# A new order of the opening work list: output-weight quarters in order of use, then the next group's keys and queries, then the values

## The chip, the cores and the metric

The kernel runs on one core of one Trainium2 chip. Its time is the device time of one execution in microseconds (us), given as the median over several executions. Five engines take part, each with its own instruction stream that runs in order: TensorE (PE, matrix products), VectorE (DVE), ScalarE (ACT, exponentials and GELU), GpSimd (POOL, masks and a part of the loads) and SyncE (SP, loads of values and stores of results). They meet only in semaphores.

## The reference

Attention with a forget gate, then a two-layer MLP. There are 8 batches, 8 heads, 576 positions, head size 64; the MLP goes from 512 to 2048 to 512 on all 4608 tokens. All inputs and the output are float32.

```
scores = scale * q @ k^T                      # per batch and head
cum    = cumsum(log(clip(f, 1e-4, 1)))
scores = where(causal, scores + cum[:, None] - cum[None, :], -1e9)
attn   = softmax(scores) @ v
x      = attn, heads side by side             # 4608 x 512
out    = gelu_tanh(x @ w_in) @ w_out
```

## The kernel before

**Attention.** Four heads form a quad; there are 16, two for each batch. The decay depends on query and key only through a factor of the key that can be pulled into the values: `make_vw` (L231) multiplies the values of a quad by exp(-cum) and writes the tile `vw`, in bfloat16. For a quad, `load_one` (L208, words LK and LQ of the lists) loads k and q with a cast to bfloat16 on POOL's DMA queue, `transpose_words` (L214, TK and TQ) transposes them on DVE, `scores` (L277, word S) multiplies them on PE in three rounds and lets ACT take the exponential into the tile `pt` (L285). Then the part of `pt` above the diagonal is set to zero, either on POOL by an affine select (L291, word M) or on DVE by a product with a 0/1 tile (L321, word m). `denominators` (word D) forms the row sums on PE (L347) and their reciprocals on DVE (L366 to L370), and `attn_out` (word V, two products for each quad) multiplies `pt` by `vw` on PE and by the reciprocals on DVE into `xT` (L379). A quad's products also need a copy of the first 64 key rows of `vw` in its last slot, at partitions 64 to 127; `copy_low` (L236, word CL) makes this edge-row copy on DVE. Tiles of k, q, `pt` and `vw` are held in two copies, for even and for odd quads.

**MLP.** Tokens go in nine chunks of 512. Words J, I, E and Q form x @ w_in and the GELU. The first chunk's second product is plain (`mlp_out`, L667, words F.0.n and f.0.n): for each of four groups of 128 tokens it adds 16 products over the rows of `w_out_sb` into a bank of PSUM (the tile `pso`), copies the bank to SBUF on DVE (L672) and stores it from SP. One word F.0.n is n of these 64 products; F uses the whole array at a time, f the same work in four strips of 32 columns. Later chunks use a scheme with seven products in place of eight on sums of blocks (L600, words F.1.n and on), for which DVE forms sums of `w_out_sb` (L567, word U), of the activations (L578 to L584, word G) and of `w_in_sb` (L450 and L452, word UW).

**Order.** There is no automatic order: `run` walks through a written list of words (`FRONT` for the first two chunks, then other lists), and each word emits its instructions, which keep that order on each engine. `@` behind a word adds a wait: the word's first load starts only when the named word's instruction is done. `load_w_out` (L201, words WO.0 to WO.3) loads a quarter of `w_out_sb`, four of the sixteen row blocks in the order in which `mlp_out` uses them, with a cast, on POOL's queue. The values of batch 1 come in five pieces of 128 positions (words LC.1.0 to LC.1.4, L185) on the same queue; those of batch 2 (words LV.2.0, LV.2.1) come on SP's queue. The words vw and VW are `make_vw` on DVE and on POOL; a second figure names a part. X loads the exponential's table on ACT.

The pools that bear on the order: `pso` lies in a pool of two banks, so the third group of 128 tokens needs the first one's copy done; the row sums and the two products of a quad share one PSUM tile (`psO`, one copy), so each needs the reader of the one before to be done.

```
psO = ctx.enter_context(tc.tile_pool(name="psO", bufs=1, space=bass.MemoryType.PSUM))
psM = ctx.enter_context(tc.tile_pool(name="psM", bufs=2, space=bass.MemoryType.PSUM))
...
def copy_low(i):
    return nc.vector.tensor_copy(vw[i % 2][64:128, LOW], vw[i % 2][0:64, 0])
...
for (key, col, q0, nq) in sorted(pieces, key=lambda x: {0: 0, "low": 1}.get(x[0], 2)):
```

The last line sets the order of the key blocks in D and V: block 0, then the edge rows, then the rest.

Of the kernel before, what the change touches and what calls it, by code (L numbers as in the profile page):

```python
# [16 lines left out]
def kernel(  # L17
# [841 lines left out]
```

## Time and profile before

| what | value |
|---|---|
| median of 3 executions | 325.47 us (323.58 to 325.6) |
| the profiled execution | 326.56 us, of which the span from first to last instruction is 324.3 us |
| PE busy | 310.0 us, 96% of the span |
| DVE, ACT, POOL busy | 241.7, 212.6, 107.0 us |
| granted TensorE clock | 1.000 of full speed |
| PE waiting for `w_out_sb` | 1.3 us in two waits |
| TK, TQ transpose on DVE | 1.25 us each |
| edge-row copy on DVE | 0.22 us each |

Times in the profile are counted from the start of the span. In a row of the timeline stand its start, its length, the engine, the line of the kernel, the operation, output<-inputs with shapes, and how many instructions are merged; in brackets the idle time of the engine before it and what ended that idle time. Matmuls are pipelined, so the length shown for a group on PE overlaps the next group by some 0.1 us.

### The profile page before, as it was taken

The numbers are of one execution on the slowest core, as the hardware profiler recorded it, in microseconds if no ns is written. First come the engines' busy times: TensorE is split into PE (matmuls) and PEld (weight loads), VectorE is DVE, ScalarE is ACT, GpSimd is POOL, SyncE is SP. The second block draws the span as 40 slices with busy tenths as digits, with TensorE's granted clock in tenths as the row PEclk, the third lists the DMA queues.
The fourth block names the chain that finished last, engine by engine and source line by source line (L and its number), as shares of the span: only waits on it lengthen the run. The fifth ranks groups of instructions, "written<-read, shape, count | busy, mean of one in ns | idle before, by whom it ended". The sixth has DMA issues, their size and how long they took to land.

```text
span 324.3 us, 11816 instructions
## 1 busy us (share of the span) xinstructions
PE 310.0 (96%) x5337; PEld 221.2 (68%) x5337; DVE 241.7 (75%) x374; ACT 212.6 (66%) x242; POOL 107.0 (33%) x145
## 2 busy tenths in 40 slices
PE   0799989999999999999999999999999999999996
PEld 0557844454677667776788877767776786788785
DVE  3664307998989978779876998599885866597574
ACT  4495667686766786678667876877587743846610
POOL 8868507253111405510752056305610150000000
PEclk9999999999999999999999999999999999999999
DMA  6999999577034951395119610981001011010202
GB/s 117 232 155 165 196 250 217 139 160 143 8 67 88 227 116 36 76 213 107 36 40 211 143 40 6 206 183 35 7 32 67 17 35 53 16 50 2 99 33 98
DMA packets 47490, 33.41 MB, mean 103 GB/s; under 512 B 29776, under 2 KB 42192, under 8 KB 47440
## 3 DMA queue, kind: packets, MB, share of 16 engines
q0 software_dynamic: 9632, 15.99, 28.4%
q1 hardware_dynamic: 37664, 16.60, 18.9%
q8 instruction: 41, 0.67, 0.8%
q14 instruction: 9, 0.07, 0.1%
q10 hardware_dynamic: 144, 0.07, 0.1%
HBM read 36.85 MB, written 9.44 MB: 143 GB/s over the span
## 4 chain that ended last, share of the span: by engine, by line
PE 82%; DMA 6%; POOL 4%; ACT 4%; DVE 2%; issue 1%; POOLq 0%; DVEq 0%
PE ps_w L600 30%; PE ps_h L395 19%; PE po L347 9%; PE ps_q L520 8%; PE ps_s L277 8%; DMA w_out_sb<-in_moe_w_out_dram 4%; PE ps_u L468 4%; PE pso L667 4%; DMA q_c<-in_q_dram 2%; ACT pt L285 2%; POOL pt L291 1%; POOL w_out_sb L201 1%; POOL v_nat L185 1%; POOL w_in_sb L197 1%; PE cum_ps L721 1%
## 5 line engine op out<-in xcount | busy, mean ns | idle before, releaser
L285 ACT ACTIVATE pt<-ps_s 128x1024 bf16<-128x1024 f32 (+2 forms) x100 | 93.9, 990 | 41.3 <-PE ps_s L277 37.1
L291 POOL TENSOR_SCALAR_AFFINE_SELECT pt<-pt 128x512 bf16<-128x512 bf16 (+3 forms) x65 | 40.8, 639 | 98.0 <-ACT pt L285 75.2
L395 PE MATMUL ps_h<-xT,w_in_sb 128*128 128x512 bf16 (+1 forms) x320 | 66.8, 358 | 0.3 <-ACT gT L403 0.2
L395 PEld LDWEIGHTS <-w_in_sb 128*128 128x128 bf16 x320 | 31.2, 98 | 26.7 <-issue 0.6
L600 PEld LDWEIGHTS <-gT 128*32 128x32 bf16 (+1 forms) x1216 | 44.2, 97 | 5.5 <-issue 2.2
L403 ACT ACTIVATE gT<-ps_h 128x1024 bf16<-128x1024 f32 x34 | 34.6, 1017 | 18.7 <-PE ps_h L395 18.4
L600 PE MATMUL ps_w<-w_out_sb,gT 128*32 128x256 bf16 (+1 forms) x1008 | 42.6, 273 | 0.0
L277 PE MATMUL ps_s<-qT,kT 32*128 32x64 bf16 (+5 forms) x896 | 36.3, 263 | 4.6 <-DVE qT L214 4.3
L600 PEld LDWEIGHTS <-gsum 128*32 128x32 bf16 (+1 forms) x948 | 35.5, 97 | 3.6 <-issue 1.3
L231 POOL TENSOR_TENSOR vw<-v_nat,wT 128x1280 bf16<-128x1280 f32 (+1 forms) x13 | 29.6, 2278 | 11.8 <-DMA v_nat<-in_v_dram 11.5
L536 DVE TENSOR_TENSOR usnap<-ps_q,usnap 128x1024 f32<-128x1024 f32 x15 | 17.9, 1222 | 18.6 <-PE ps_q L520 13.2
L277 PEld LDWEIGHTS <-kT 32*128 32x128 bf16 x896 | 16.5, 93 | 20.9 <-issue 11.5
L600 PE MATMUL ps_w<-usum,gsum 128*32 128x256 bf16 (+1 forms) x791 | 29.9, 273 | 0.0
L617 DVE COPY snap<-ps_w 128x512 f32<-128x512 f32 x32 | 21.8, 681 | 6.1 <-PE ps_w L600 6.0
L531 ACT ACTIVATE gT<-usnap 128x1024 bf16<-128x1024 f32 x15 | 15.8, 1054 | 12.1 <-DVE usnap L536 11.8
L379 DVE TENSOR_TENSOR xT<-po,rb 128x576 bf16<-128x576 f32 x26 | 19.5, 752 | 5.6 <-PE po L347 5.3
L347 PE MATMUL po<-pt,vw 128*32 128x64 bf16 (+4 forms) x624 | 22.4, 278 | 0.0
L214 DVE STREAM_TRANSPOSE qT<-q_c 128x576 f32<-128x576 f32 x16 | 19.8, 1247 | 2.7 <-DMA q_c<-in_q_dram 2.5
L214 DVE STREAM_TRANSPOSE kT<-k_c 128x576 f32<-128x576 f32 x16 | 19.5, 1248 | 3.1 <-DMA k_c<-in_k_dram 3.1
L347 PEld LDWEIGHTS <-vw 128*32 128x32 bf16 x672 | 14.8, 97 | 9.3 <-issue 2.8
L208 POOL DMA_DIRECT2D k_c<-in_k_dram x16 | 9.1, 569 | 33.7 <-DVE kT L214 17.4
L520 PEld LDWEIGHTS <-w_in_sb 128*128 128x128 bf16 x160 | 15.6, 98 | 2.5 <-issue 0.4
(134 smaller groups left out, 478.4 us busy)
## 6 DMA issues: line engine op xcount, KB each, us to landing
out_dram<-o_st SPq DMA_DIRECT2D x35, 256.0 KB, 2.3
k_c<-in_k_dram POOLq DMA_DIRECT2D x16, 288.0 KB, 5.2
q_c<-in_q_dram POOLq DMA_DIRECT2D x16, 288.0 KB, 6.2
v_nat<-in_v_dram SPq DMA_DIRECT2D x16, 256.0 KB, 5.3
v_nat<-in_v_dram SPq DMA_DIRECT2D x20, 128.0 KB, 4.9
v_nat<-in_v_dram POOLq DMA_DIRECT2D x8, 256.0 KB, 8.2
w_in_sb<-in_moe_w_in_dram POOLq DMA_DIRECT2D x8, 256.0 KB, 7.6
w_out_sb<-in_moe_w_out_dram POOLq DMA_DIRECT2D x4, 512.0 KB, 11.1
```

What stands on the lines that cost most here:

```text
L214: return nc.vector.transpose(out=dst.rearrange("p s c -> p (s c)").bitcast(FP32) .rearrange("p (t a) -> p a t", a=S // 32), in_=src.rearra ...
L231: return eng.tensor_mul(vw[i % 2][:, t0:t1], vb[:, t0:t1, h0:h0 + 4, :], wT[:, i, t0:t1, :].unsqueeze(3).to_broadcast([128, t1 - t0, 4, D]))
L277: nc.tensor.matmul(tiles[h // 2][:, h % 2, c0:c0 + nq], key_columns(i, key, h, c), qq[32 * h:32 * h + 32, q0:q0 + nq, c], start=(c == 0 an ...
L285: nc.scalar.activation(p[:, 2 * g:2 * g + 2, off:off + n], t[:, :, 0:n], AF.Exp, scale=scale)
L291: nc.gpsimd.affine_select(out=x, in_=x, compare_op=ALU.is_ge, fill=0.0, base=0, pattern=pattern, channel_multiplier=-1)
L347: nc.tensor.matmul(po[r0:r0 + w.shape[-1], 448 + q0:448 + q0 + nq], w, p[:, h, col:col + nq], start=(key in (0, "low")), stop=(key in ("lo ...
L379: nc.vector.tensor_mul(xT[:, 2 * u + x, r0 + s0:r0 + s1], po, rbs[i, part])
L395: nc.tensor.matmul(ph[:, j, n * cols:(n + 1) * cols], w_in_sb[:, dt, 128 * ft:128 * ft + 128], xT[:, dt, h0:h0 + cols], start=(dt == 0 and ...
L403: nc.scalar.activation(gelus(c, 2 * pr, 2), ph, AF.Gelu_apprx_tanh)
L520: nc.tensor.matmul(ps[:, k, HC * n:HC * n + HC], w[:, d, 128 * n:128 * n + 128], x[:, d, :], start=(first and n == 0 and d == 0), stop=(d ...
L600: nc.tensor.matmul(ps[c0:c0 + width, n, cols[0]:cols[1]], x[:, j, 128 * n + c0:128 * n + c0 + width], w[:, j, cols[0]:cols[1]], start=(fir ...
L617: copy(kept[name], ps)
```

## The change

Only the list `FRONT` changes. The four quarters of `w_out` are issued on POOL's queue in the order 0, 1, 2, 3 with no values between them; behind them come k and q of quad 3, and behind these the remaining four pieces of the values of batch 1 (before: quarter 0, values 2, quarters 2 and 1, values 0, quarter 3, values 1 and 3, then k and q of quad 3). TQ.3 moves ahead of the first group's copy on DVE, beside TK.3. The mask of quad 2's second round moves from DVE (m.2.1) to POOL (M.2.1) and stands, with the other masks of that quad, ahead of VW.3, which was ahead of them. CL.2 and CL.3 now follow D.2 together; before, CL.2 stood ahead of D.2 and CL.3 after V.2.1. The products of the first chunk (F.0.n, f.0.n) are cut in other portions between the attention's words. UW.2.1, UW.2.2, m.4.1, VW.4 and some words of the I group change place by a few words, and LV.3.1 waits for LQ.7 in place of LK.6.

```diff
         WI.7 LK.2 V.1.1.0 m.0.3.2 H.1.3.0 j.0.0 vw.0.1 H.1.3.1 LC.1.4 m.0.3.4 D.0.1 M.1.3 S.1.2 M.1.1 VW.1.1 V.0.0.1 WO.0 V.0.1.1 LC.1.2 D.1.1
-        WO.2@m.0.3.4 J.0.1 J.0.2 WO.1 LC.1.0@VW.1.1 WO.3@m.0.3.2 V.1.0.1 V.1.1.1 LC.1.1 GJ.0.0 LC.1.3 TK.2 J.1.1 LK.3 J.0.3 J.1.0 LQ.3 TQ.2 LQ.4 VW.3
-        J.1.3 LK.4 J.1.2 F.0.4 X F.0.4 S.2.0 F.0.11 TK.3 S.2.2 F.0.6 LV.2.0 TQ.3 F.0.4 LK.5 S.2.1 F.0.2 F.0.7 TQ.4 m.2.1 S.3.0 vw.2 CL.2 M.2.2 f.0.7
-        M.2.0 D.2 S.3.1 f.0.7 LQ.5 V.2.0 m.3.0 S.3.2 TK.4 LK.6@LQ.4 f.0.1 f.0.3 V.2.1 M.3.2 f.0.2 S.4.1 CL.3 m.3.1 LQ.6 f.0.5 TQ.5 H.4.2.1 D.3 H.4.0.1
-        H.4.0.0 VW.4 V.3.1 v.3.0 f.0.1 H.4.2.0 U.0 m.4.1 LV.2.1@m.3.1 I.1.1 LQ.7@CL.3 I.1.4 TQ.6 I.1.6 m.4.2.3 I.1.0 m.4.2.2 I.1.5 CL.4 U.3 LV.3.0@LQ.7
-        U.1 TK.6 I.1.2 M.4.0 U.2 G.0 TK.5 UW.2.1 I.1.3 I.1.7 G.1.1.2 F.1.16 X UW.2.2 S.5.0 UW.2.3 LQ.8 F.1.19 S.5.1 D.4 VW.5 M.5.0 f.1.13 S.5.2 V.4.0
+        ... V.0.0.1 WO.0 V.0.1.1 D.1.1 WO.1@m.0.3.4
+        J.0.1 J.0.2 WO.2 WO.3 LK.3 LQ.3 V.1.0.1 V.1.1.1 LC.1.2 LC.1.0@m.0.3.4 LC.1.3 GJ.0.0 LC.1.1 TK.2 J.1.1 J.0.3 TQ.2 J.1.0 J.1.3 LQ.4 LK.4 J.1.2
+        F.0.4 F.0.5 X TK.3 TQ.3 S.2.0 F.0.11 S.2.2 F.0.10 LV.2.0 LK.5 S.2.1 F.0.9 vw.2 S.3.0 TQ.4 F.0.8 M.2.2 M.2.0 M.2.1 D.2 VW.3 S.3.1 CL.2 CL.3 F.0.6
+        LQ.5 V.2.0 m.3.0 TK.4 S.3.2 LK.6@LQ.4 f.0.2 M.3.2 V.2.1 F.0.1 f.0.2 S.4.1 m.3.1 LQ.6 F.0.5 TQ.5 H.4.2.1 D.3 H.4.0.1 H.4.0.0 V.3.1 v.3.0
+        f.0.1 H.4.2.0 VW.4 m.4.1 U.0 LV.2.1@m.3.1 I.1.1 I.1.4 LQ.7@CL.3 UW.2.1 TQ.6 I.1.6 I.1.0 m.4.2.3 m.4.2.2 I.1.5 CL.4 U.3 LV.3.0@LQ.7 U.1 I.1.2
+        TK.6 M.4.0 U.2 I.1.3 I.1.7 G.0 TK.5 G.1.1.2 X UW.2.2 F.1.16 S.5.0 UW.2.3 LQ.8 F.1.19 S.5.1 D.4 VW.5 M.5.0 f.1.13 S.5.2 V.4.0 f.1.14 V.4.1
...
-        LV.3.1@LK.6 f.1.5 CL.6 LK.8 m.6.2.3
+        ... V.5.0 LV.3.1@LQ.7 f.1.5 CL.6 LK.8 m.6.2.3
```

More of the change, by code (lines that the diff above doesn't have):

```diff
@@ L77 @@
         WI.5 H.1.0.0 D.0.0 M.1.0.1 M.1.0.0 H.0.1.1 V.0.0.0 H.0.1.0 M.0.1 LQ.2 V.0.1.0 B.1.256 H.1.1.0 D.1.0 WI.4 H.0.3.0 WI.6 B.1.256 V.1.0.0 H.0.3.1
-        WI.7 LK.2 V.1.1.0 m.0.3.2 H.1.3.0 j.0.0 vw.0.1 H.1.3.1 LC.1.4 m.0.3.4 D.0.1 M.1.3 S.1.2 M.1.1 VW.1.1 V.0.0.1 WO.0 V.0.1.1 LC.1.2 D.1.1
-        WO.2@m.0.3.4 J.0.1 J.0.2 WO.1 LC.1.0@VW.1.1 WO.3@m.0.3.2 V.1.0.1 V.1.1.1 LC.1.1 GJ.0.0 LC.1.3 TK.2 J.1.1 LK.3 J.0.3 J.1.0 LQ.3 TQ.2 LQ.4 VW.3
-        J.1.3 LK.4 J.1.2 F.0.4 X F.0.4 S.2.0 F.0.11 TK.3 S.2.2 F.0.6 LV.2.0 TQ.3 F.0.4 LK.5 S.2.1 F.0.2 F.0.7 TQ.4 m.2.1 S.3.0 vw.2 CL.2 M.2.2 f.0.7
-        M.2.0 D.2 S.3.1 f.0.7 LQ.5 V.2.0 m.3.0 S.3.2 TK.4 LK.6@LQ.4 f.0.1 f.0.3 V.2.1 M.3.2 f.0.2 S.4.1 CL.3 m.3.1 LQ.6 f.0.5 TQ.5 H.4.2.1 D.3 H.4.0.1
-        H.4.0.0 VW.4 V.3.1 v.3.0 f.0.1 H.4.2.0 U.0 m.4.1 LV.2.1@m.3.1 I.1.1 LQ.7@CL.3 I.1.4 TQ.6 I.1.6 m.4.2.3 I.1.0 m.4.2.2 I.1.5 CL.4 U.3 LV.3.0@LQ.7
-        U.1 TK.6 I.1.2 M.4.0 U.2 G.0 TK.5 UW.2.1 I.1.3 I.1.7 G.1.1.2 F.1.16 X UW.2.2 S.5.0 UW.2.3 LQ.8 F.1.19 S.5.1 D.4 VW.5 M.5.0 f.1.13 S.5.2 V.4.0
-        f.1.14 V.4.1 UW.2.4 m.5.2.3 m.5.2.2 CL.5 M.5.1 S.6.0 f.1.13 D.5 S.6.1 f.1.4 LK.7 V.5.1 f.1.3 f.1.10 vw.6 S.6.2 m.6.1 M.6.2.2 m.6.0 V.5.0
-        LV.3.1@LK.6 f.1.5 CL.6 LK.8 m.6.2.3
+        WI.7 LK.2 V.1.1.0 m.0.3.2 H.1.3.0 j.0.0 vw.0.1 H.1.3.1 LC.1.4 m.0.3.4 D.0.1 M.1.3 S.1.2 M.1.1 VW.1.1 V.0.0.1 WO.0 V.0.1.1 D.1.1 WO.1@m.0.3.4
+        J.0.1 J.0.2 WO.2 WO.3 LK.3 LQ.3 V.1.0.1 V.1.1.1 LC.1.2 LC.1.0@m.0.3.4 LC.1.3 GJ.0.0 LC.1.1 TK.2 J.1.1 J.0.3 TQ.2 J.1.0 J.1.3 LQ.4 LK.4 J.1.2
[3 more added lines that the diff above has]
+        TK.6 M.4.0 U.2 I.1.3 I.1.7 G.0 TK.5 G.1.1.2 X UW.2.2 F.1.16 S.5.0 UW.2.3 LQ.8 F.1.19 S.5.1 D.4 VW.5 M.5.0 f.1.13 S.5.2 V.4.0 f.1.14 V.4.1
+        UW.2.4 m.5.2.3 m.5.2.2 CL.5 M.5.1 S.6.0 f.1.13 D.5 S.6.1 f.1.4 LK.7 V.5.1 f.1.3 f.1.10 vw.6 S.6.2 m.6.1 M.6.2.2 m.6.0 V.5.0 LV.3.1@LQ.7 f.1.5
+        CL.6 LK.8 m.6.2.3
     """
```

## The prediction

> **What bounds the kernel now.** I began with the page: engines, then the chain that ended last.
>
> ```profile
> span 324.3 us, 11816 instructions
> PE 310.0 (96%) x5337; PEld 221.2 (68%) x5337; DVE 241.7 (75%) x374; ACT 212.6 (66%) x242; POOL 107.0 (33%) x145
> ...
> PE 82%; DMA 6%; POOL 4%; ACT 4%; DVE 2%; issue 1%; POOLq 0%; DVEq 0%
> ```
>
> PE is the bound. Of its 14.3 us of idle, 9.1 lie in two waits before 9.9 us (4.75 and 4.35), which the change does not touch. The list of waits from 30 us on leaves one that counts, and PE's timeline gives its place:
>
> ```profile
> PE pso L667 <- DMA w_out_sb<-in_moe_w_out_dram: 1.3, 2, 0.7
> ```
>
> ```profile
> 43.58 1.02 PE L667 MATMUL pso<-w_out_sb,gT 128*128 128x512 bf16 x4 [0.60 <-DMA w_out_sb<-in_moe_w_out_dram]
> ...
> 46.86 1.67 PE L667 MATMUL pso<-w_out_sb,gT 128*128 128x512 bf16 x7 [0.66 <-DMA w_out_sb<-in_moe_w_out_dram]
> ```
>
> PE stands 0.60 us for quarter 1, which was issued third, and 0.66 for quarter 3, issued at 33.16 and landed at 46.82 (the chain in order of time has this load as its piece of 13.66). So 1.26 us is about all that a better order can win; everything else is what new waits it makes. Issue start plus time to landing, from the DMA view window by window, gives the queue's order:
>
> ```profile
> w_out_sb<-in_moe_w_out_dram POOLq DMA_DIRECT2D x1, 512.0 KB, 8.1
> ...
> w_out_sb<-in_moe_w_out_dram POOLq DMA_DIRECT2D x1, 512.0 KB, 13.7
> ...
> v_nat<-in_v_dram POOLq DMA_DIRECT2D x2, 256.0 KB, 13.5
> ```
>
> The first line is quarter 0, the second quarter 3, the third the last two value pieces. Landings before: quarter 0 at 29.09+8.1=37.2, values 2 at 29.90+8.1=38.0, quarter 2 at 30.79+10.2=41.0, quarter 1 at 31.5+12.0=43.5, values 0 at 32.27+12.1=44.4, quarter 3 46.8, values 1 and 3 at 33.91 and 34.8 with 13.5 to 13.6 in 47.5 and 48.3, k of quad 3 at 37.48+12.1=49.6, q of quad 3 at 38.24+12.8=51.0, q of quad 4 at 41.56+10.9=52.5. They land in order of issue, so differences are prices: a quarter 3.0, 2.5, 2.4; a value piece 0.7 to 0.9; a k or q tile 1.3 to 1.5.
>
> **The loads in the new order.** Quarter 0 keeps its issue and its landing at 37.2. The other three cost 7.9 together: quarter 3 at 45.1 (44.4 with all at 2.4, 46.2 with all at 3.0), quarter 2 near 42.4. Then k of quad 3 46.5, q 47.9, four value pieces at 0.8 end at 51.1, q of quad 4 at 52.6: the bytes ahead of that one are the same as before. POOL's issues must keep up: before, it stood 1.75 us until 37.48 and 2.78 until 41.56, each time for the load eight places back. By that count LC.1.3 goes at 37.4, LC.1.1 at 40.2, LQ.4 at 42.6, LK.4 at 45.3, all ahead of their turn. LK.5 waits for TK.3 (46.5+1.25=47.8) and is out by 48.4; behind it on POOL stand quad 2's masks, of which the first can't start before 49.75.
>
> **PE walked with its own rows.** F portions cost 0.228 a product (2.05 for 9 in the chain), f 0.231 (1.62 for 7), so F for f is free. From 41.95: F.0.4 and F.0.5 2.05 to 44.0 (block 8, quarter 2, is wanted at 43.8, landed 42.4); S.2.0 0.65; F.0.11 wants quarter 3 at 44.65+0.68=45.3, landed 45.1, no wait, and ends at 47.1, where S.2.2 starts: 48.47 before, so **-1.35**. S.2.2 0.57, F.0.10 2.27, S.2.1 0.57, F.0.9 2.05, S.3.0 0.67, F.0.8 1.82: D.2 at 55.1 (56.10 before). D.2 0.68, S.3.1 0.57, F.0.6 1.37: V.2.0 ready at 57.7 (58.97 before).
>
> **DVE behind D.2: where some is given back.**
>
> ```profile
> 57.01 0.78 DVE L366 STREAM_TRANSPOSE den<-po 128x576 f32<-128x576 f32 x1 [0.53 <-PE po L347]
> ...
> 58.13 0.78 DVE L370 STREAM_TRANSPOSE rb<-rec 128x576 f32<-128x576 f32 x1
> ...
> 59.88 0.76 DVE L379 TENSOR_TENSOR xT<-po,rb 128x576 bf16<-128x576 f32 x1 [0.40 <-PE po L347]
> ```
>
> Row sums start 0.91 behind D.2 and take 1.90: 56.0 to 57.9. Before, CL.2 was done by 56.5; now it runs 57.9 to 58.1, and V.2.0 wants the edge rows right after block 0 (57.7+0.22): PE stands 0.2 to 0.25. CL.3 (0.25) and the copy of the third group (0.68) run to 59.05, then xT of V.2.0 to 59.8. V.2.1 writes the same PSUM tile: ready 58.65+0.57+0.5=59.7, free 59.85, stands 0.15, ends 60.55. m.3.0 (0.35) and TK.4 (1.25) follow xT on DVE: kT at 61.4; S.4.1 is ready at 60.55+0.8=61.35 and starts 61.4 against 62.41 in PE's timeline before: **-1.0**. F.0.5 1.19, H.4.2.1 0.56: D.3 at 63.7 against 64.73. What follows D.3 is the same list on PE, up to I.1.1 at 68.1 (69.14 before), and from there PE is full (64 products in 13.97).
>
> **What lies beside other work.** TQ.3 ahead of the first copy: copied by 47.9+1.25+0.7=49.85; the third group wants that bank at 50.5+0.45=50.95, cover 1.1; LV.2.0 goes behind that store on SP, 1.2 later than 49.04, its last piece lands about 60.5 (59.3 before), VW.4 wants it at 63.9. M.2.1 on POOL costs 0.65 (mean of that form) and frees 0.41 on DVE: M.2.2 when the exponential ends (49.75), M.2.0, then M.2.1 52.55 to 53.2; D.2 wants it at 55.1, cover 1.9. VW.3 then 53.2 to 55.5; CL.3, which stands on DVE at 58.1, has 2.6 of cover; if that is gone, copy, xT of V.2.0, m.3.0 and TK.4 queue behind CL.3 and V.2.1 and S.4.1 wait us for us. vw.2 runs from 51.65 (second copy done) to 53.1 with values at 51.1; TQ.4 to 54.35; row sums want DVE at 56.0, cover 1.6. LQ.5 is issued at 55.5 in place of 54.11 and lands near 61 (6.5 before), TQ.5 wants it at 62.5. LK.6 waits for TK.4 as before; M.3.2 behind it 61.95 to 63.35, D.3 at 63.7, cover 0.35. UW.2.1 (0.41) falls into the 1.24 us for which DVE waits ahead of G.0 at 79.02; UW.2.2 changes places with it; with no cover, 0.41 against g2's first reader at 87.17, 1.2 behind its writer. Gates: LC.1.0's m.0.3.4 is done by 29, LV.3.1 goes on SP near 101 when LQ.7 (67.23+4.0) and LK.6 have both landed. VW.4 keeps its place on POOL. All nothing.
>
> **Sum.** -1.26 (waits), -0.1 (portions), +0.35 (CL.2, PSUM tile, kT): -1.0 on the profiled execution, 326.56 (324.3 span and 2.26 around it) to 325.5. That execution is 1.1 above the median 325.47, so **324.4** for the median. Bounds of the unknowns: quarter 3 at 46.2 gives back 0.9; DVE's give-back is 0 to 0.8.
>
> **A lock between DVE and POOL.** vw.2 now falls beside masks. DVE's timeline, and POOL's row beside its second line:
>
> ```profile
> 63.15 0.78 DVE L321 TENSOR_TENSOR pt<-pt,causal 128x512 bf16<-128x512 bf16 x1
> ...
> 79.02 2.16 DVE L578 TENSOR_TENSOR gsum<-gT 128x1024 bf16<-128x1024 bf16 x1 [1.24 <-ACT gT L403]
> ...
> 84.58 0.66 DVE L578 TENSOR_TENSOR gsum<-gT 128x1024 bf16<-128x1024 bf16 x1
> ```
>
> ```profile
> 78.31 2.33 POOL L231 TENSOR_TENSOR vw<-v_nat,wT 128x1280 bf16<-128x1280 f32 x1 [5.15 <-DMA v_nat<-in_v_dram]
> ```
>
> The mask product takes 0.41 at 54.42 with POOL idle and 0.78 at 63.15 beside POOL's masks (63.02 to 64.42); the same sum 0.66 alone and 2.16 beside a weighted value on POOL, ending 0.5 after it. So a two-operand DVE instruction seems to wait for the POOL instruction that is running: up to 0.65 beside a mask, within vw.2's cover of 1.6, and up to 2.33 beside VW.3, which now stands close to vw.2: the third rival. [...]
>
> [...]
>
> **Rivals.** (1) *The last quarter is still late*: three quarters at 3.0. For it: quarter 2 did take 3.0. Against: the next two took 2.5 and 2.4. 0.9 of the 1.26 stays; with the give-back, -0.1: 325.4. Here the reordering doesn't do what it says. (2) *No give-back*: CL.2 and the PSUM tile cost nothing, because DVE's queue runs 0.4 earlier than walked; -1.4: 324.0. For it: DVE is idle 0.53 ahead of the row sums and 0.40 ahead of xT before. Against: 1.90 of rows between D.2 and CL.2, which no order of the loads shortens. (3) *Values too late*, slower: values land after 53.2, so that vw.2 and VW.3 start together and POOL gets the lock; landing L, vw.2 ends at L+2.33+1.47, TQ.4 at L+5.05. With L=53.2 the row sums start 2.3 late, V.2.0 stands 2.6 in place of 0.25: +1.4, 326.9; with L=54.6 (LC.1.1 at 41.1 and the 13.5 of the rows) +2.8, 328.3. It decides from 53.2, 2.1 later than walked. For it: values are last in a queue that is full until 59, and the two multiplies have the same start condition. Against: the bytes ahead of them sum to 51.1.
>
> **Chances.** Forecast 0.60 (323.9 to 325.2 around 324.4), rival 1 0.12, rival 2 0.08, rival 3 0.20. The measurement tells about 1% (3.25 us) from no change. Faster by that needs more idle than PE has here: 0.03, for scatter (the three runs lie 2.0 apart). Slower: three quarters of rival 3, as L may go past its bound with new waits behind it: 0.15. Same: 0.82. The range of 8 in 10 leaves out the far half of rival 3 and the lower scatter: 323.1 to 327.6.
>
> **What would show it.** Right: no wait of L667 for w_out; S.2.2 near 47.1, D.2 near 55.1, I.1.1 near 68.1; the masks of quad 2 ahead of VW.3, ended by 53.2; CL.2 right behind the row sums, and PE idle 0.2 to 0.4 in V.2.0 and V.2.1; TQ.4 ended before D.2. Wrong: PE waiting for w_out near 45; vw.2 or CL.3 longer than their rows or begun after 53; D.2 standing for M.2.1; any new wait of L277 for kT or qT over 0.5 us; span not within 322.5 to 324.2.

## The result, and the profile after

The changed kernel takes 328.25 us (median of six executions, 327.41 to 328.73), the kernel before 325.28 beside it (six, 323.58 to 325.83): ratio 1.0096, interval 1.0068 to 1.0124, so about 3 us slower. The forecast was 324.4, with a range up to 327.6. The profiled execution took 328.7. First the page:

```profile
span 326.9 us, 11667 instructions
...
PE 310.7 (95%) x5255; PEld 221.2 (68%) x5274; DVE 245.0 (75%) x373; ACT 212.7 (65%) x242; POOL 108.8 (33%) x146
...
PE 88%; DVE 5%; ACT 3%; DMA 2%; issue 1%; POOL 0%; DVEq 0%; POOLq 0%
```

DMA's share of the chain fell from 6% to 2%, DVE's rose from 2% to 5%, and DVE is busy 3.3 us more with one instruction fewer (m.2.1 went to POOL). PE's waits name the place (time in all, times, longest):

```profile
PE ps_lt L700 <- ACT f_all L695: 4.8, 1, 4.8
PE ps_s L277 <- DVE qT L214: 2.9, 1, 2.9
PE po L347 <- DVE pt L321: 2.2, 1, 2.2
...
PE po L347 <- DVE den L366: 0.3, 1, 0.3
```

The waits for `w_out` are gone, as forecast. In their place stands one of 2.2 us for a mask product on DVE (L321). In the timelines of DVE, POOL and PE:

```profile
60.65 0.74 DVE L379 TENSOR_TENSOR xT<-po,rb 128x576 bf16<-128x576 f32 x1
61.32 4.71 DVE L321 TENSOR_TENSOR pt<-pt,causal 128x512 bf16<-128x512 bf16 x1
65.95 1.24 DVE L214 STREAM_TRANSPOSE qT<-q_c 128x576 f32<-128x576 f32 x1
67.05 0.73 DVE L366 STREAM_TRANSPOSE den<-po 128x576 f32<-128x576 f32 x1
```

```profile
61.11 0.53 POOL L208 DMA_DIRECT2D k_c<-in_k_dram  x1 [4.60 <-DVE kT L214]
61.64 1.23 POOL L291 TENSOR_SCALAR_AFFINE_SELECT pt<-pt 128x512 bf16<-128x512 bf16 x2
62.82 0.55 POOL L208 DMA_DIRECT2D q_c<-in_q_dram  x1
63.39 2.34 POOL L231 TENSOR_TENSOR vw<-v_nat,wT 128x1280 bf16<-128x1280 f32 x1
```

```profile
63.45 0.43 PE L347 MATMUL po<-pt,w_bf 128*32 128x512 bf16 x8
66.08 0.61 PE L347 MATMUL po<-pt,w_bf 128*1 128x448 bf16 x16 [2.20 <-DVE pt L321]
...
67.83 1.53 PE L347 MATMUL po<-pt,vw 128*32 128x512 bf16 x24 [0.27 <-DVE den L366]
69.14 1.56 PE L347 MATMUL ps_o<-pt,vw 128*32 128x512 bf16 x24
```

The mask product of quad 3 (m.3.1) takes 4.71 us; the same form takes 0.41 elsewhere. The start of such a row is read here as the moment at which the instruction asks to run, and what the row has over its usual length as standing. It asks 0.21 us into POOL's issue of LK.6 and ends 0.3 after VW.4: it stood through the issue, both edge masks, a second issue and a weighted value. In the kernel before, the same stretch of DVE and POOL reads:

```profile
62.90 0.22 DVE L236 COPY vw<-vw 64x256 bf16<-64x256 bf16 x1
63.15 0.78 DVE L321 TENSOR_TENSOR pt<-pt,causal 128x512 bf16<-128x512 bf16 x1
```

```profile
62.44 0.53 POOL L208 DMA_DIRECT2D k_c<-in_k_dram  x1 [7.78 <-ACT pt L285]
63.02 1.40 POOL L291 TENSOR_SCALAR_AFFINE_SELECT pt<-pt 128x512 bf16<-128x512 bf16 x2
```

There CL.3 asks 0.46 into the issue and takes its usual 0.22, and m.3.1 asks during the first mask and gets in ahead of the second: the two masks take 1.40 together in place of 1.23. In the change D.3, which starts at 63.45, wants m.3.1's result. The products of quad 3 behind it take 1.53 and 1.56 in place of 0.87 and 0.87, and the windows of one microsecond say why (stretch; length; busy time of PE, PEld, DVE, ACT, POOL; granted clock; DMA share; GB/s):

```profile
67.00:68.00 1.00, 0.73 (x26) 0.40 (x18) 0.96 (x3) 0.65 (x1) 0.51 (x1) 0.92 0.07 16
68.00:69.00 1.00, 1.00 (x20) 0.52 (x16) 0.86 (x2) 1.00 (x2) 0.09 (x1) 0.50 0.25 25
69.00:70.00 1.00, 1.00 (x25) 0.57 (x21) 0.59 (x1) 0.29 (x1) 0.56 (x2) 0.50 0.95 154
70.00:71.00 1.00, 1.00 (x20) 0.51 (x12) 0.42 (x2) 0.00 (x0) 0.51 (x1) 0.50 0.63 113
71.00:72.00 1.00, 1.00 (x13) 0.51 (x11) 1.00 (x2) 0.21 (x1) 0.00 (x0) 0.88 0.01 2
```

The clock falls to half from 67.83 to 71.25. The stall brought it on: before, and in the seven runs below without such a wait of PE, the mean granted clock of the profiled execution is 0.999 or 1.000, and of the twelve profiles with a wait of 2.2 us or more (this one and eleven runs below) eleven show such a fall (means of 0.990 to 0.995).

**Where the time went.** From D.3 to I.1.1 PE needs 8.23 us against 4.41: 2.20 and 0.27 of waits, 1.66 of rows lengthened by the half clock (V.3.1 0.66, v.3.0 0.69, the output product 0.25, a scores group 0.06), less 0.3 elsewhere. D.3 itself started 1.28 earlier than before, of which 0.32 is only that this execution reached F.0.4 sooner (41.63 against 41.95). So the change wins 0.96 up to D.3 and loses 3.82 behind it. From I.1.1 to the end both take the same (255.2 us).

### The profile page after: what moved, and what is told of

It is laid out like the page before. It is cut to its first block, busy times and chain, and to the rows that moved or that the text cites. A ratio compares the mean times of both kernels' runs of the same rounds, so it can differ in the third digit from the quotient of the medians.

```text
span 326.9 us, 11667 instructions
## 1 busy us (share of the span) xinstructions
PE 310.7 (95%) x5255; PEld 221.2 (68%) x5274; DVE 245.0 (75%) x373; ACT 212.7 (65%) x242; POOL 108.8 (33%) x146
## 4 chain that ended last, share of the span: by engine, by line
PE 88%; DVE 5%; ACT 3%; DMA 2%; issue 1%; POOL 0%; DVEq 0%; POOLq 0%
PE ps_w L600 30%; PE ps_h L395 18%; PE po L347 9%; PE ps_s L277 9%; PE ps_q L520 8%; PE ps_h L419 4%; PE ps_u L468 4%; PE pso L667 3%; DMA q_c<-in_q_dram 2%; DVE pt L321 2%; PE po_m L333 1%; ACT pt L285 1%; DVE qT L214 1%; PE cum_ps L721 1%; PE ps_o L347 1%
## 5 line engine op out<-in xcount | busy, mean ns | idle before, releaser
L291 POOL TENSOR_SCALAR_AFFINE_SELECT pt<-pt 128x512 bf16<-128x512 bf16 (+3 forms) x66 | 41.9, 646 | 101.9 <-ACT pt L285 79.2
L395 PE MATMUL ps_h<-xT,w_in_sb 128*128 128x512 bf16 (+1 forms) x307 | 65.7, 357 | 1.0 <-ACT gT L403 0.2
L347 PE MATMUL po<-pt,vw 128*32 128x64 bf16 (+4 forms) x624 | 23.2, 284 | 0.3 <-DVE den L366 0.3
## 6 DMA issues: line engine op xcount, KB each, us to landing
out_dram<-o_st SPq DMA_DIRECT2D x35, 256.0 KB, 2.4
v_nat<-in_v_dram SPq DMA_DIRECT2D x16, 256.0 KB, 5.5
v_nat<-in_v_dram POOLq DMA_DIRECT2D x8, 256.0 KB, 9.4
w_in_sb<-in_moe_w_in_dram POOLq DMA_DIRECT2D x8, 256.0 KB, 7.6
```

What stands on the lines that cost most here:

```text
L291: nc.gpsimd.affine_select(out=x, in_=x, compare_op=ALU.is_ge, fill=0.0, base=0, pattern=pattern, channel_multiplier=-1)
L347: nc.tensor.matmul(po[r0:r0 + w.shape[-1], 448 + q0:448 + q0 + nq], w, p[:, h, col:col + nq], start=(key in (0, "low")), stop=(key in ("lo ...
L395: nc.tensor.matmul(ph[:, j, n * cols:(n + 1) * cols], w_in_sb[:, dt, 128 * ft:128 * ft + 128], xT[:, dt, h0:h0 + cols], start=(dt == 0 and ...
```

## The experiments

Edits are of the list `FRONT` unless said otherwise. "D.3 to I.1.1" is not comparable where words move, so for the front I use F.0.4's start to I.1.1's: 27.2 before, 30.05 after.

**1. The mask product early** (`e1_mask_early`, on the change).

```diff
-LQ.5 V.2.0 m.3.0 TK.4 ... S.4.1 m.3.1 LQ.6
+LQ.5 V.2.0 m.3.0 m.3.1 TK.4 ... S.4.1 LQ.6
```

> The changed kernel with one word moved: DVE's product mask of quad 3's second round (m.3.1) stands right behind m.3.0, ahead of TK.4, where POOL is idle. Theory A (in the changed kernel m.3.1 is shut out by POOL's unbroken run of load issue, two masks, load issue and weighted value, 4.71 us in place of 0.41, and PE stands for it): m.3.1 takes 0.4 us near 59.6, no wait of D.3 over 0.2 us, TensorE's granted clock 1.00 throughout, I.1.1 near 68.0 to 68.4 us, time 1.0 us (0.3 to 1.4) below the kernel before: ratio 0.996 to 0.999. Rival B (the long row is only where a late input shows; the cost comes from the new order of the loads): still 327 to 328.5 us, ratio 1.006 to 1.011, with the wait at another place.

Measured: 324.76 us, ratio 0.9992 (0.9972 to 1.0012), front 26.34, clock 1.00. Both products now run ahead of POOL's run:

```profile
59.40 0.75 DVE L321 TENSOR_TENSOR pt<-pt,causal 128x512 bf16<-128x512 bf16 x2
```

With this one word moved the whole loss is gone, with the loads as the change has them. So the loss is m.3.1's, and the loads cost nothing.

**2. The edge-row copy back** (`e2_edge_back`, on the change): CL.3 back to between S.4.1 and m.3.1.

```diff
-CL.2 CL.3 F.0.6 ... S.4.1 m.3.1
+CL.2 F.0.6 ... S.4.1 CL.3 m.3.1
```

> The changed kernel with the edge-row copy of quad 3 (CL.3) back ahead of m.3.1, nothing else. Theory A1 (what decides is the instant at which m.3.1 asks: with CL.3's 0.25 us ahead it asks after POOL's load issue, during the first mask, and gets in behind that mask as in the kernel before): m.3.1 0.8 us, ratio 0.996 to 0.999. Theory A2 (the place does not matter, any request ahead of an unbroken run on POOL loses until the run ends): m.3.1 still over 4 us, ratio 1.006 to 1.011. Rival B (loads): ratio 1.006 to 1.011 with m.3.1 short.

Measured: 328.67, ratio 1.0119 (1.0087 to 1.0152), wait of PE 2.5. Now the copy takes the blow, and m.3.1 0.43 behind it:

```profile
60.59 4.41 DVE L236 COPY vw<-vw 64x256 bf16<-64x256 bf16 x1
```

In this kernel whichever of the two asks during LK.6's issue is shut out. Moving CL.3 is not the cause.

**3. Both copies together in the kernel before** (`e3_before_edges`): CL.3 directly behind CL.2, all else as before.

```diff
-vw.2 CL.2 M.2.2 ... S.4.1 CL.3 m.3.1
+vw.2 CL.2 CL.3 M.2.2 ... S.4.1 m.3.1
```

> The kernel before with one word moved: CL.3 stands right behind CL.2, so m.3.1 follows the attention product directly and asks near 62.9 us, inside POOL's load issue of 62.44 to 62.97. Theory A1: m.3.1 is shut out to the end of the weighted value on POOL (67.3) and takes 4 to 4.7 us; PE stands about 2 us in D.3, the granted clock falls for some us behind it, time 3 to 4 us above the kernel before, ratio 1.009 to 1.013. Theory A2: the same. Rival B: nothing, ratio 0.998 to 1.002, as the loads are those of the kernel before.

Measured: 324.05, ratio 0.9994 (0.9972 to 1.0016). m.3.1 asks 0.34 into LK.6's issue (60.33) and is let in:

```profile
60.67 0.42 DVE L321 TENSOR_TENSOR pt<-pt,causal 128x512 bf16<-128x512 bf16 x1
```

So, against both theories, asking during the issue is not enough. PE waits 0.7 for `w_out` here, 1.3 in the profile of before with the same loads: that term varies between executions (1.5 and 1.9 in runs 6 and 16).

**4. The change's POOL queue in the kernel before** (`e4_before_loads`): its loads, and VW.3 behind the masks; DVE's order of before, with m.2.1 still on DVE.

```diff
-WO.2@m.0.3.4 ... WO.1 LC.1.0@VW.1.1 WO.3@m.0.3.2 ... LK.3 ... LQ.3 TQ.2 LQ.4 VW.3 ... M.2.0 D.2 S.3.1
+WO.1@m.0.3.4 ... WO.2 WO.3 LK.3 LQ.3 ... LC.1.2 LC.1.0@m.0.3.4 LC.1.3 GJ.0.0 LC.1.1 TK.2 ... LQ.4 ... M.2.0 D.2 VW.3 S.3.1
```

> The kernel before with POOL's queue of the change alone (quarters 0 to 3, k and q of quad 3, then the values; VW.3 behind the masks of quad 2), every word of DVE in its old order, m.2.1 still on DVE, CL.3 in its old place. Theory A: the waits of PE for w_out fall from 1.26 us to at most 0.3, m.3.1 takes 0.8 us, ratio 0.995 to 0.998. Rival B (loads cost): ratio above 1.004, and a wait for kT, qT or the weighted values of quad 2 shows between 47 and 62 us.

Measured: 328.44, ratio 1.0119 (1.0092 to 1.0147); CL.3 takes 4.40, PE waits 2.7 for m.3.1 behind it, and none for `w_out`. These two changes of POOL's queue bring the whole loss without any change of DVE's order.

**5. The transpose first** (`e5_transpose_first`, on the change): TQ.5 ahead of m.3.1.

```diff
-S.4.1 m.3.1 LQ.6 F.0.5 TQ.5
+S.4.1 LQ.6 TQ.5 m.3.1 F.0.5
```

> The changed kernel with TQ.5 ahead of m.3.1 on DVE, POOL's list untouched, so the mask product asks some 1.1 us later, inside POOL's second mask, and not inside the load issue of LK.6. Theory A3 (a DVE instruction from SBUF to SBUF that asks in the first 0.3 us of a load issue on POOL is shut out until POOL's run of instructions pauses; one that asks inside a mask or a weighted value gets in behind that one instruction): m.3.1 0.4 to 1.0 us near 62.4, no wait of D.3 over 0.3 us, granted clock 1.00, ratio 0.997 to 1.001. Theory A2 (any request ahead of an unbroken run loses until the run ends near 65.7): m.3.1 about 3.3 us, ratio 1.007 to 1.012.

Measured: 327.99, ratio 1.0087 (1.0058 to 1.0116). TQ.5 had to stand 0.76 for its load, so m.3.1 asked at 62.76, within LQ.6's issue (62.33 to 62.88), and took 2.77: past VW.4, ready behind that issue. The moment I meant to hit was missed, but the second issue shuts out like the first.

**6. Another moment in the kernel before** (`e6_before_product_early`): on PE, f.0.3 behind V.2.1.

```diff
-f.0.1 f.0.3 V.2.1 M.3.2
+f.0.1 V.2.1 f.0.3 M.3.2
```

> The kernel before with one move on PE alone: three products f.0.3 stand behind V.2.1 in place of ahead of it. V.2.1's product is then done when DVE ends TK.4, its multiplication follows TK.4 without a gap, and CL.3 asks 0.3 us after LK.6's issue starts in place of 0.46. Theory A3: CL.3 is shut out for 4 to 4.5 us up to the end of the weighted value on POOL, PE stands 2 to 3 us in D.3, granted clock 0.99 to 0.995, ratio 1.008 to 1.013, with the loads, DVE's order and POOL's order of the kernel before. If the order of words by itself decides, and not the instant: CL.3 0.22 us and ratio 0.998 to 1.002.

Measured: 325.18, ratio 1.0003 (0.9981 to 1.0026). CL.3 asks 0.32 into LK.6's issue, the same moment as in run 2, and takes 0.23. The moment of asking doesn't decide.

**7. The weighted value later** (`e7_value_later`, on the change): VW.4 behind LQ.7 on POOL, so that no ready computation follows LQ.6.

```diff
-H.4.2.0 VW.4 m.4.1 ... LQ.7@CL.3 UW.2.1
+H.4.2.0 m.4.1 ... LQ.7@CL.3 VW.4 UW.2.1
```

> The changed kernel with POOL's VW.4 behind LQ.7. LQ.7 waits for TQ.5, which stands behind m.3.1 on DVE, so POOL pauses after LQ.6 near 63.4. Theory A3: m.3.1 is still shut out by LK.6, the two masks and LQ.6, but now ends near 63.8: 2.2 to 2.6 us in place of 4.71; PE stands 0.3 to 0.8 us in D.3; the granted clock stays at 1.00; ratio 0.998 to 1.004. If the row of 4.71 is another wait that only looks like POOL's: the row stays over 4 us and the ratio at 1.006 to 1.011.

Measured: 324.55, ratio 0.9988 (0.9972 to 1.0004), front 26.22, clock 1.00:

```profile
60.83 1.84 DVE L321 TENSOR_TENSOR pt<-pt,causal 128x512 bf16<-128x512 bf16 x1
```

```profile
60.62 0.53 POOL L208 DMA_DIRECT2D k_c<-in_k_dram  x1 [4.06 <-DVE kT L214]
61.16 1.23 POOL L291 TENSOR_SCALAR_AFFINE_SELECT pt<-pt 128x512 bf16<-128x512 bf16 x2
62.34 0.55 POOL L208 DMA_DIRECT2D q_c<-in_q_dram  x1
64.14 0.53 POOL L208 DMA_DIRECT2D q_c<-in_q_dram  x1 [1.26 <-DVE qT L214]
```

m.3.1 ends at 62.67, 0.3 after the masks and inside LQ.6's issue. It asked as early as in the change; it now stands only for the masks. So the price at this place is the length of POOL's unbroken run of ready instructions behind the issue, further issues inside it included.

**8. Both cures in the fourth kernel** (`e8_loads_masks_early`): run 4 with m.3.1 behind m.3.0 and CL.3 behind V.2.0.

```diff
-LQ.5 V.2.0 m.3.0 S.3.2 ... S.4.1 CL.3 m.3.1 LQ.6
+LQ.5 V.2.0 CL.3 m.3.0 m.3.1 S.3.2 ... S.4.1 LQ.6
```

> The kernel before with POOL's queue of the change (the loads in the new order, VW.3 behind the masks of quad 2) and with m.3.1 behind m.3.0 and CL.3 behind the multiplication of V.2.0, where POOL is idle; CL.2 keeps its old place ahead of D.2. This is the loads' order with the lock taken out. Theory A: m.3.1 and CL.3 take their 0.4 and 0.2 us, no wait for w_out, from F.0.4 to I.1.1 26.0 to 26.5 us against 27.2 in the profile before and 26.6 in that of the moved edge copy, ratio 0.995 to 0.999. Rival B (the loads cost by themselves): ratio above 1.003.

Measured: 325.92, ratio 1.0006 (0.9985 to 1.0027). No instruction is shut out, but PE stands 0.9 for kT and 0.5 for a mask, since DVE does more ahead of TK.4; the front is 27.2, not 26.0 to 26.5, so the gain expected of the loads is not shown here.

**9 and 10. Which part of POOL's queue?** Before, the first edge mask of quad 3 (M.3.2) also waits for an older instruction of POOL's own; behind the moved VW.3 that wait is not needed. `e9_old_wait` puts one back on the change (there, and in runs 15, 17 and 18, `mask` also returns its instructions so that the list can hang a wait on them). `e10_value_alone` moves only VW.3, with the loads of before.

```diff
-f.0.2 M.3.2 V.2.1
+f.0.2 M.3.2@VW.3 V.2.1        # e9, on the change
```
```diff
-TQ.2 LQ.4 VW.3 J.1.3 ... M.2.0 D.2 S.3.1
+TQ.2 LQ.4 J.1.3 ... M.2.0 D.2 VW.3 S.3.1        # e10, on the kernel before
```

> The changed kernel, its orders untouched, with one thing more: the first edge mask of quad 3 on GpSimd (behind the issue of k of quad 6) also waits for the weighted value of quad 3, GpSimd's own instruction of some 5 us before, so the wait is satisfied when it is reached. The kernel before had such a wait on GpSimd's own queue at this mask, and a gap of 0.05 us between the issue and the mask in its trace; the change moved it onto the masks of quad 2, and the gap is gone. Theory C (a VectorE instruction that asks while GpSimd issues a load is let in only where the next GpSimd instruction is not ready yet): the gap of about 0.05 us comes back, the mask product of quad 3 takes at most 0.8 us instead of 4.71, TensorE's waits of 2.20 and 0.27 us are gone, the row sums' successor starts some 2.5 to 3.5 us earlier, ratio 0.996 to 1.001 to the kernel before. Rival (the wait is a bystander; it is the length of GpSimd's unbroken run of masks, load and weighted value alone): the product still takes over 4 us, ratio 1.007 to 1.012, 327.7 to 329.2 us.

> The kernel before with one move only: the weighted value of quad 3 goes from ahead of the masks of quad 2 to behind them on GpSimd, as in the change; the loads of w_out, k, q and v, and VectorE's order, stay as before. GpSimd's first edge mask of quad 3 thereby loses its wait for GpSimd's own earlier work. Theory C: the edge-row copy of quad 3 or the mask product behind it, whichever asks while k of quad 6 is issued, takes 4.2 to 4.8 us, TensorE waits 2 to 3 us in quad 3's product, granted clock falls below 1.00 there, ratio 1.007 to 1.013. Rival (the new order of the loads is needed for it, by when the tiles land): no VectorE instruction over 1 us at this place, ratio 0.998 to 1.003.

Measured: e9 327.52, ratio 1.0095 (1.0078 to 1.0113); m.3.1 4.72, no gap ahead of the mask (59.86 + 0.53 = 60.39, then 60.40). The wait is a bystander. e10 329.34, ratio 1.0162 (1.0135 to 1.0188), and

```profile
62.75 4.41 DVE L236 COPY vw<-vw 64x256 bf16<-64x256 bf16 x1
```

One word moved on POOL is enough to bring the stall. Two things in its profile may make e10 dearer than the change: PE still waits 0.7 for `w_out`, and vw.2, now beside VW.3, takes 3.62.

**11. Both cures on the change** (`e11_both`): the edits of runs 1 and 7 together.

> The changed kernel with the mask product of quad 3 moved behind the one of its low columns, ahead of the transpose of k of quad 4 (as in the run with the early mask), and with the weighted value of quad 4 behind the load of q of quad 7 on GpSimd (as in the run with the later value). If the two runs' gains are of the same stall, they do not add: 324.2 to 325.0 us, ratio 0.996 to 1.000. If the change's own saving at w_out (1.0 us by the walk) was still hidden in each by the other's rest, 323.6 to 324.2, ratio 0.993 to 0.997. If the later value is late for its product, a new wait there and ratio above 1.000.

Measured: 324.49, ratio 0.9990 (0.9970 to 1.0010), front 26.34. They don't add: it was one stall. It is no proven gain on the kernel before, and neither is run 7.

**12 to 14. What of the queue?** A small mask (64 columns of a tile that nothing else reads, 0.23 us) behind VW.3 in the change; a small product (0.32 us) behind the masks of quad 2 in the kernel before; the small mask close ahead of LK.6 in the kernel before.

```diff
-D.2 VW.3 S.3.1
+D.2 VW.3 PB S.3.1             # e12, on the change
-M.2.0 D.2 S.3.1
+M.2.0 D.2 PQ S.3.1            # e13, on the kernel before
-m.3.0 S.3.2 TK.4
+m.3.0 S.3.2 PB@m.3.0 TK.4     # e14, on the kernel before
...
+"PB": lambda: nc.gpsimd.affine_select(out=probe, in_=probe, compare_op=ALU.is_ge, fill=0.0, base=0, ...),
+"PQ": lambda: nc.gpsimd.tensor_mul(probe, utri_f32[:, 0:64], utri_f32[:, 64:128]),
```

> The changed kernel with one small instruction more on GpSimd: a mask of the same kind (affine select) over 64 columns of a tile that nothing else reads, directly behind the weighted value of quad 3. GpSimd's last computation before the load of k of quad 6 and the edge masks of quad 3 is thereby a mask again, as in the kernel before, and not the weighted value; GpSimd's idle time ahead of that load stays some 4 us. Theory D (what counts is the kind of GpSimd's last computation: behind one of the same kind the next mask begins some 0.05 us after the issue, and a VectorE instruction that asks during the issue is let in): the mask product of quad 3 takes at most 0.8 us, ratio 0.996 to 1.001. Rival E (what counts is how long GpSimd has computed nothing: 8.9 us in the three runs that let VectorE in, 4.6 to 8.0 us in those that did not): still over 4 us, ratio 1.007 to 1.012.

> The kernel before with one small instruction more on GpSimd: a product of two constant 128x64 fp32 tiles into a tile that nothing else reads, directly behind the masks of quad 2, ahead of the load of q of quad 5. GpSimd's last computation before the edge masks of quad 3 is thereby a product, as in the changed kernel; loads and VectorE's order stay as before, and GpSimd computes nothing for some 8.5 us after it. Theory D: the edge-row copy of quad 3 or the mask product behind it takes 4.2 to 4.8 us, ratio 1.007 to 1.014, TensorE waits 2 to 3 us in quad 3's product. Rival E: neither takes over 0.8 us, ratio 0.998 to 1.003.

> The kernel before with one small mask (affine select over 64 columns of a tile that nothing else reads) on GpSimd behind the load of q of quad 5, which waits for VectorE's product of the low-column mask of quad 3, so that GpSimd computes about 1.5 us before the load of k of quad 6. Theory D: the kind is the same, VectorE is let in as before: copy and product at most 0.8 us, ratio 0.998 to 1.003. Rival E (a short idle time of GpSimd shuts VectorE out): copy or product over 4 us, ratio 1.007 to 1.014.

Measured: e12 328.52, ratio 1.0108 (1.0069 to 1.0147), m.3.1 4.71; e13 329.0, ratio 1.0112 (1.0073 to 1.0152), CL.3 4.27; e14 328.41, ratio 1.0107 (1.0066 to 1.0148), CL.3 4.28. All three are shut out. The kind falls with e12 and e14 (a mask was last, and VectorE lost). The idle time fits e12 and e14 and is not excluded by e13: ahead of the mask behind LK.6, POOL had computed nothing for 8.4 us there, and for 8.8 to 8.9 in the three profiles that let VectorE in. In e13 and e14 one instruction (0.32 and 0.23 us), whose result nothing waits for, costs the kernel 1.1%.

**15 to 18. Joint conditions.**

```diff
-V.2.1 M.3.2 f.0.2
+V.2.1 M.3.2@VW.3 f.0.2        # e15, on the kernel of run 10
-f.0.1 f.0.3 V.2.1 ... vw.2 CL.2 M.2.2 ... CL.3 m.3.1
+f.0.1 V.2.1 f.0.3 ... vw.2 CL.2 CL.3 M.2.2 ... m.3.1     # e16, on the kernel before
-f.0.2 M.3.2 V.2.1
+f.0.2 M.3.2@VW.3 V.2.1        # e17, on the kernel of run 2
-f.0.2 M.3.2 V.2.1
+f.0.2 M.3.2@PB V.2.1          # e18, on the kernel of run 12
```

> The kernel before with the weighted value of quad 3 moved behind the masks of quad 2 on GpSimd (the run with the value alone), and with the satisfied wait for that value added at the first edge mask of quad 3 (the run with the old wait). VectorE's order is that of before, so the edge-row copy of quad 3 asks some 0.32 us into the issue of k of quad 6. Theory G (VectorE gets in if two things hold: the mask has such a wait, which the trace shows as a separate semaphore instruction of GpSimd ahead of the load, and VectorE asks at least 0.3 us into the issue; with the wait alone, in the run with the old wait, it asked at 0.21 and lost): copy and mask product at most 0.8 us, ratio 0.998 to 1.004. Rival H (something else in the kernel before's GpSimd queue, such as the place in its stream, lets VectorE in there): copy 4.2 to 4.8 us, ratio 1.008 to 1.017.

> The kernel before, GpSimd's queue untouched (its mask has the wait), with both edge-row copies of quads 2 and 3 together and the attention product of quad 2 ahead of the extra seven units of the output product on TensorE, so that the mask product of quad 3 asks some 0.21 us into the issue of k of quad 6, not at 0.32 to 0.46. Theory G: asked before 0.3 us, it is shut out as in the run with the old wait: mask product 4.4 to 4.8 us, ratio 1.007 to 1.012. Rival H: GpSimd's queue decides, so it is let in: at most 0.8 us, ratio 0.997 to 1.002.

> The changed kernel with the edge-row copy of quad 3 back ahead of the mask product (the run with the edge back, 1.012), and the satisfied wait for the weighted value at the first edge mask of quad 3. The copy asks 0.32 us into the issue of k of quad 6. Theory G: it is let in, the stall is gone and the change's own saving is left: ratio 0.996 to 1.001. Rival H: copy over 4 us, ratio 1.008 to 1.013.

> The changed kernel with two things on GpSimd that each changed nothing alone: the small mask behind the weighted value of quad 3 (the run with the small mask), and a satisfied wait for GpSimd's last computation at the first edge mask of quad 3 (the run with the old wait), here for that small mask. Theory I (VectorE gets in where both hold, as in the four runs in which it did: the last computation is a mask, and the edge mask has the wait; runs with one of the two lost): mask product at most 0.8 us, the gap of 0.05 us ahead of the mask is back, ratio 0.996 to 1.001. Rival J (something else in the kernel before's untouched GpSimd queue decides): mask product over 4 us, ratio 1.007 to 1.013.

Measured: e15 329.6, ratio 1.0146 (1.0099 to 1.0192); e17 329.32, 1.0146 (1.0099 to 1.0193); e18 328.49, 1.0116 (1.0079 to 1.0154). PE's longest wait for m.3.1's tile is 2.7, 2.5 and 2.2, the same as in runs 10, 2 and 12, on whose kernels they stand. e16 325.38, 1.0012 (0.9989 to 1.0034), with POOL's queue of before:

```profile
61.79 0.40 DVE L321 TENSOR_TENSOR pt<-pt,causal 128x512 bf16<-128x512 bf16 x1
```

```profile
61.58 0.53 POOL L208 DMA_DIRECT2D k_c<-in_k_dram  x1 [7.75 <-ACT pt L285]
62.17 1.22 POOL L291 TENSOR_SCALAR_AFFINE_SELECT pt<-pt 128x512 bf16<-128x512 bf16 x2
```

It asks 0.21 into the issue, as m.3.1 does in the change, and is let in; the mask begins 0.06 behind the issue's end. All my joint conditions fall. In four profiles (before and runs 3, 6 and 16) VectorE was let in; they share POOL's queue of before, untouched. In the thirteen with any change to that queue in which VectorE asked during one of the two issues (after and runs 2, 4, 5, 7, 9, 10, 12 to 15, 17 and 18), it was shut out (in 15, 17 and 18 by the sign of PE's wait), in run 7 by the masks and in run 5 by the weighted value alone. Which property of the queue it is stays open: not the loads (runs 10, 13 and 14 have those of before), the wait, the kind of the last computation or the moment. The time for which POOL had computed nothing ahead of LK.6's masks does part those in which it was read, 8.8 to 8.9 us in the four against 1.65 (run 14) to 8.4 (run 13) in the change and runs 2, 4, 5, 7, 9, 10 and 12 to 14, but no run lengthened or shortened it with nothing else changed, so that it decides is not shown.

## Why the prediction was wrong

**Right: the loads and PE's walk.** Quarter 3 made no wait (in run 12, with the same loads, one of 0.7 came back: the walked margin of 0.2 is thin). It landed at 44.9 (predicted: 45.1), and that by two misses that nearly cancel: quarter 0 landed at 35.8 in place of 37.2, and the three behind it took 9.1 in place of 7.9. k and q of quad 3 landed at 46.3 and 47.9 (46.5 and 47.9), the last value piece at 51.2 (51.1), q of quad 4 at 52.6 (52.6). With the 0.32 by which this execution started sooner added, PE's starts are S.2.2 47.10 (47.1), D.2 55.04 (55.1), V.2.0 57.80 (57.7), S.4.1 61.40 (61.4) and D.3 63.77 (63.7):

```profile
46.78 0.63 PE L277 MATMUL ps_s<-qT,kT 32*128 32x320 bf16 x16
...
54.72 0.87 PE L347 MATMUL po<-pt,w_bf 128*32 128x512 bf16 x24
...
57.48 1.01 PE L347 MATMUL po<-pt,vw 128*32 128x512 bf16 x24
```

The give-back showed where it was put: V.2.0's row stretches to 1.01 (0.85 before) as it stands for CL.2. The -1.0 up to D.3 is there.

**The step that failed: "What lies beside other work".** Of what stands between S.4.1 and D.3 it gave cover to M.3.2 alone (0.35), whose masks did end in time, at 62.87. m.3.1, which D.3 wants as well, got no term. By the walk's own rows (kT at 61.4, then 0.7 for the xT of V.2.1) it would begin at 62.1, 1.6 us ahead of D.3: enough for 0.41, and for the 0.78 that it took before. It took 4.71. The row that should have warned stood in the prediction, m.3.1's 0.78 beside POOL's masks, with 2.3 us of VW.4 ready behind them. Nor does any of the prediction's signs of being wrong name m.3.1.

**The rule inside it: "seems to wait for the POOL instruction that is running".** That capped a loss at 0.65 beside a mask and 2.33 beside a weighted value. For a DVE instruction that asks while POOL issues a load and is shut out, the runs show another cap, the whole run of ready instructions behind that issue: two masks in run 7 (1.84), issue and weighted value in run 5 (2.77), all of it in the change (4.71). In the change the mask product asked 0.32 before POOL's mask began (61.32 against 61.64), during a load's issue, and lost to every instruction in turn.

For a DVE instruction that asks while POOL computes, the rule held where it was read. In the profiles of before, the change and runs 4 to 8 a sum of activations asks during a later weighted value with a mask ready behind it, three times over, and takes 1.31 or 1.32 each time; the first in the change:

```profile
160.50 1.31 DVE L582 TENSOR_TENSOR gT<-gT 128x1024 bf16<-128x1024 bf16 x1
```

```profile
158.93 2.33 POOL L231 TENSOR_TENSOR vw<-v_nat,wT 128x1280 bf16<-128x1280 f32 x1
161.22 1.09 POOL L291 TENSOR_SCALAR_AFFINE_SELECT pt<-pt 128x512 bf16<-128x512 bf16 x1
```

The sum (0.67 alone) waits for the weighted value only and gets in ahead of the mask, whose row is 1.09 long in place of 0.64. So the rule was drawn from rows of one kind and used where the other kind was to come. The prediction had a row of that other kind and misread it: it gives the 0.41 at 54.42 as "with POOL idle", but POOL was issuing LQ.5 then (54.11, for 0.55), with no ready instruction behind it.

**Rival 3** had the right kind of mechanism, a slower kernel through this lock, but at vw.2 and VW.3 through late values; that its 326.9 to 328.3 holds the measured time is chance. The values came in time: vw.2 asked at 51.43 and took 1.74, its 1.47 and 0.27 behind a mask. It was a place away: moving VW.3 behind the masks of quad 2, costed at nothing because VW.3 itself had cover, is by itself enough to bring the loss (run 10). Whether the new order of the loads alone would bring it too was not run.

**What was left out of the sum:** the clock. A stall of 2.2 us was priced at most us for us; behind it PE ran 3.41 us at half speed, 1.66 more.

**The gain itself is smaller than -1.0.** With the stall away the ratios are 0.9992, 0.9988 and 0.9990 (runs 1, 7, 11), 0.26 to 0.39 us of 325; -1.0 would be 0.9969, just outside all three intervals. The profiled execution of before, 326.56, lies above every timed one beside the change, so a gain against it (front 27.2 to 26.3, -0.85) looks larger than against the median; in run 3, with the loads of before, the front is 26.56. How much each of these carries is not settled.

## What to carry to other kernels

Before moving an instruction on GpSimd, write out what VectorE does on SBUF beside the whole unbroken run of GpSimd instructions behind it, load issues included. A VectorE instruction that asked while GpSimd computed waited here for that one instruction (a sum took 1.31 us in place of 0.67); one that asked while GpSimd issued a load could lose the length of the whole ready run behind the issue (a mask product took 4.71 in place of 0.41), and is to be priced at that. Whether it does lose, no rule found here foretells. The cure is cheap: put the short VectorE instruction that PE waits for ahead of the run, or break the run with an instruction that isn't ready yet; both took the whole loss away here (ratios 0.9992 and 0.9988). A wait of PE of some 2 us may cost nearly as much again in the clock (1.66 us behind waits of 2.47 in the change), so a forecast for a stall needs two terms.

## What the runs showed of the hardware that I had not expected

**A shut-out that crosses load issues.** VectorE and GpSimd do not meet in semaphores alone: a VectorE copy of 0.22 us took 4.27 to 4.41, a mask product of 0.41 up to 4.72, through issue, masks, issue and weighted value. GpSimd loses too: with VectorE first, VW.3 took 3.64 in run 2 and 3.56 in run 7, against 2.33, and M.2.1 1.31 in the change, against 0.65. Transposes of 32-bit words (TQ.5, 1.25 beside the masks of run 3) and products that read PSUM (xT, 0.76 beside VW.4 in run 7) kept their length.

**The clock falls in steps of one length.** In the change the trace's record of the granted clock has full speed for 54.61 us up to the fall at 67.83, half for 3.41 and full for the next 256.0; in the kernel before it has full speed for 310.61. These are 16, 1, 75 and 91 times 3.413. One step at half speed makes a mean of 0.995 over the span, two make 0.990: the profiled executions of runs 2, 4, 5, 9, 10, 13, 15 and 17 have 0.993 to 0.995, those of runs 14 and 18 0.990, and the windows of run 18 add up to 6.8 us at half speed. The profiled execution of run 12 has 0.998, less than one step's loss, though PE's wait there was 2.2 as in the change; three other executions of that kernel have 0.990 to 0.995, and one each of runs 4 and 9 has 1.000. So a kernel with such a stall pays for a spell in most of its executions and not in all. Whether it goes by where the stall lies among the steps is not shown, nor why the spell is two steps long in runs 14 and 18. The step ahead of the fall in the change (64.42 to 67.83) holds 1.93 us in which PE stands and 1.48 in which it works, so that much standing, with work around it, was enough here.
